# A fused attention, mixer and MLP kernel on one core: the MLP in five blocks of 924 tokens in one pass, with its Strassen weight slices streamed from HBM

## The chip, the core and the metric

The kernel runs on one core of a Trainium2 chip. The metric is the device time of one execution in microseconds (us). Engines are named as in the profile: PE (TensorE matmuls), PEld (its weight loads), DVE (VectorE), ACT (ScalarE), POOL (GpSimd), SP (SyncE, which issues most of the DMAs).

## The reference, cut to what matters

```python
attn_out = _attn_ref(...)                  # feature-map attention, 8 x 8 heads x 576 x 64
x = attn_out.transpose(0, 2, 1, 3).reshape(B, S, H * D)      # 8 x 576 x 512
x = (gate(x) * (x @ w_val)) @ w_out        # gate: sigmoid of a causal convolution of 5 taps
mixed = real(fft(fft(x, axis=1), axis=2))
u = x + mixed
un = (u - mean(u)) / sqrt(var(u) + 1e-6)   # over the 512 features
out = u + maximum(un @ w_ch1, 0) @ w_ch2   # 512 -> 2048 -> 512
```

## The kernel before, in words

**Stages.** The attention (to about 313 us) is scheduled by hand in `run_attention`; beside it the MLP's weights are converted from float64 and written to the HBM scratch `w_scr`. Then come the mixer and the FFT as matmuls ("the mixing", to about 608 us), batch after batch: `note_V` (value, tile `val`), `note_W` (w_out), `note_FD` and `note_SD` (the transforms), which leaves u in the scratch `u_scr`. Then the MLP, to the end.

**Order.** From the mixing on, the functions `note_...`, `ln_stages`, `prep_un`, `c1_units` and `c2_units` only record operations with what they read and write. `place_ops` (line 1112) then plans all of them: each has costs per engine (`COST`, line 617), a due time counted back from the end along its successors and along PE's work, and of the operations that are ready the one due first is placed. Operations recorded for "vp" can go to DVE or POOL. The result is a fixed order of instructions on each engine; each engine runs its own in order. Tiles live in five parts (`STAGES`, line 620) whose memory is opened and closed one after the other.

**Precision.** Every float32 operand is split into a rounded high part and a remainder, and a product takes three float32r matmuls: high by high, high by low, low by high. A split is a copy on ACT (`o_hi`) and a subtraction on DVE or POOL (`o_lo`).

**Strassen.** Both MLP products use a form of Strassen's algorithm with 7 products in place of 8. The weight side needs 7 slices per 2 x 2 quadrant block: three are quadrants themselves and four are sums, which `note_sums` (line 375) computes during the mixing in 32 steps (load of 256 KB, four sums of 128 columns, store of 256 KB; two buffers `ws`). `prep_w` (line 662) later loads them and splits them into resident tiles `w`. The token side needs 7 operands `un`, made by `prep_un` (line 770): 4 sums, 7 high parts, 7 low parts.

**The MLP.** 4608 tokens stand as 9 blocks of 512 (two halves of `HB` = 256 columns). The weights of half the hidden units fit, so there are two passes over the blocks, 18 visits: pass 0 with the first half, partial sums kept in `part_scr` and normalised tokens in `un_scr`, and pass 1 backwards with the other half. A visit has two rounds c. In a round `c1_units` (line 799) has 7 units of 12 matmuls of 256 columns (tiles x, y, z) with the Strassen additions, the ReLU and the splits into `h` after them, 14 vector operations of 512 columns; `c2_units` (line 874) has 7 units of 12 matmuls of 256 columns into cx, cy and cz, each but one added to `acc` on DVE. The c2 of a round runs interleaved with the c1 of the next. In pass 0 the LayerNorm of the next block (`ln_stages`, line 713) runs beside; that of block 0 is recorded in the mixing after batch 4. `note_mlp` (line 1072) records all this.

Of the kernel before, what the change touches and what calls it, by code (L numbers as in the profile page):

```python
# [8 lines left out]
F32 = mybir.dt.float32  # L9
# [11 lines left out]
NT = NB * S  # L21
# [3 lines left out]
TB = 512  # L25
HB = TB // 2
NBK = NT // TB
# [38 lines left out]
def attention_moe_mixer_kernel(  # L66
# [92 lines left out]
    w_scr = [dram.tile([NJ, 2, 128, 8 * 128], F32, name=f"w_scr{i}") for i in range(2)]  # L159
    un_scr = [dram.tile([128, 4, TB], F32, name=f"un_scr{t}") for t in range(NBK)]  # L160
    part_scr = [[dram.tile([128, 2, HB], F32, name=f"part_scr{t}_{q}") for q in range(4)] for t in range(NBK)]
    u_scr = [dram.tile([4, 128, S], F32, name=f"u_scr{b}") for b in range(NB)]

    keep = pool(ctx, "keep", 1)
    wo_all = keep.tile([128, 2, 4 * DM], F32R, name="wo")
    wo = [wo_all[:, i].rearrange("p (c f) -> p c f", f=DM) for i in range(2)]
    P = {"g1": pool(ctx, "g1", 1)}

    mix = ExitStack()
# [22 lines left out]
    late["s1"] = ln_p.tile([128, TB], F32, name="s1")  # L192
    late["A"] = ln_p.tile([128, 4, TB], F32, name="A")
# [176 lines left out]
    def conv_mlp(n, j, i):  # L370
        def done(t):
            nc.sync.dma_start(out=w_scr[i][j][:, :, 0:512].rearrange("o p f -> p o f"), in_=t)
        return convert(n, (w_ch1, w_ch2)[i][j].bitcast(I32).rearrange("o p f -> p o f"), 1024, (2,), False, done)

    def note_sums(n):
        i, j, o = wsteps[n]
        b = ("ws", n % 2)
        t = later(b)
        a21, a11, a12, a22 = (t[:, k * 128:(k + 1) * 128] for k in range(4))
        k21, k11, k12, k22 = keys = [b + (k,) for k in range(4)]  # L380
        o_dma([(t, w_scr[i][j, o][:, 0:512])], [], keys, 256)
        o_tt("vp", a22, a21, a22, ALU.add, 128, [k21, k22], [k22])
        o_tt("vp", a21, a11, a21, ALU.subtract, 128, [k11, k21], [k21])
        o_tt("vp", a11, a22, a11, ALU.subtract, 128, [k22, k11], [k11])
        o_tt("vp", a12, a12, a11, ALU.subtract, 128, [k12, k11], [k12])
        o_dma([(w_scr[i][j, o][:, 512:1024], t)], keys, [("w_scr", i, j, o)], 256)
# [26 lines left out]
    def open_mix():  # L413
# [7 lines left out]
        for i in range(2):  # L421
            late["ws", i] = ws.tile([128, 512], F32, name=f"ws{i}")
            late["pv", i] = psv.tile([128, NE + 2], F32, name=f"val{i}")
            late["gv", i] = P["g"].tile([128, NE], F32, tag="gv", name="gv")
            late["gs", i] = P["g"].tile([128, 2, NE], F32, tag="gs", name="gs")
        late["pa"] = psa.tile([128, 2, 512], F32, name="acc")

    def open_mix2():
# [3 lines left out]
        late["u"] = x2.tile([128, 4, S], F32, name="u")  # L432
        late["u256"] = x2.tile([97, S], F32, name="u256")
# [3 lines left out]
        for i in range(2):  # L437
# [4 lines left out]
            late["T0", i] = x2.tile([128, 2, HB], F32, name=f"T0{i}")  # L442
            late[("sh0", "sl0")[i]] = x2.tile([128, HB], F32R, name=("sh0", "sl0")[i])
        for i in range(4):
            late["ps", i] = ps.tile([128, 512], F32, name=f"ps{i}")
# [12 lines left out]
    wsteps = [(i, j, o) for j in range(NJ) for i in range(2) for o in range(2)]  # L458
# [52 lines left out]
    def note_V(b, m):  # L511
# [4 lines left out]
        for n in range(2):  # L516
# [3 lines left out]
            def prod(e, p=p, sl=sl):  # L520
                ws = slice(m * 128, (m + 1) * 128)
                for c in range(4):
                    mm3(p[:, 0:NE], (wv[0][:, c, ws], wv[1][:, c, ws]), (h[:, c, sl], l[:, c, sl]), c == 0, c == 3)
            op("m", 0, prod, [("xh", c, k) for c in range(4) for k in range(2)], [("pv", n)], 12 * 0.134)
# [21 lines left out]
    NJP = NJ // 2  # L546
    NH_SLOTS = 7
    blocks = [(0, t) for t in range(NBK)] + [(1, t) for t in reversed(range(NBK))]
    wt = [[], []]
    wr = []  # L550
    un_op = []
    hs = []
    h_more = []
# [4 lines left out]
    def w_tiles(p, i, j):  # L558
        return [[p.tile([128, 7, 128], F32R, name=f"w{i}_{j}_{o}_{k}") for k in range(2)] for o in range(2)]

    def w_views(t):
# [908 lines left out]
```

## Time and profile before

| what | us |
|---|---|
| median of 3 runs | 1380.53 (1379.85 to 1385.03) |
| the profiled execution | 1378.82 |
| span of its trace, first to last instruction | 1377.0 |
| PE busy in the span | 1330.1 (97%) |
| DVE busy | 1183.7 (86%) |
| ACT busy | 820.5 (60%) |
| POOL busy | 582.0 (42%) |

The span is what the trace shows; the execution's own time is 1.8 us longer. Busy times are unions of the instructions' durations. On PE a matmul's duration runs on past the start of the next one, so that its pace is read from start to start.

### The profile page before, as it was taken

How to read it: one execution, taken by the hardware profiler on the slowest of the kernel's cores; microseconds unless marked ns; L12 is line 12 of the kernel's file. 1: busy time of each engine (PE TensorE's matmuls, PEld its weight loads, DVE VectorE, ACT ScalarE, POOL GpSimd, SP SyncE). 2: the span in 40 equal slices, each digit the busy share in tenths (PEclk: the TensorE clock that was granted, in tenths of full speed). 3: DMA queues.
4: the chain of work that ended last, by engine and by line, in shares of the span. 5: the costliest groups of instructions: out<-in, count | busy, mean ns of one | idle time of the engine just before them, and what ended most of it. 6: DMA issues, size and time to landing. Idle time of an engine off the chain costs nothing.

```text
span 1377.0 us, 35052 instructions
## 1 busy us (share of the span) xinstructions
PE 1330.1 (97%) x14672; PEld 1288.3 (94%) x14672; DVE 1183.7 (86%) x2006; ACT 820.5 (60%) x1554; POOL 582.0 (42%) x452
## 2 busy tenths in 40 slices
PE   8999999997999999996999999999999999999998
PEld 7888888887999999996999999999999999999998
DVE  7999999887889999887899999999897777777776
ACT  6888888865555546465565565555565445544542
POOL 3978888613666654342533234343223111111110
PEclk9999999998999999998999999999999999999999
DMA  7477777643444440144422333222543212222211
GB/s 266 144 278 272 272 266 263 223 159 121 144 161 161 162 146 35 66 151 167 161 85 85 119 97 123 94 77 77 177 122 105 77 62 78 93 62 92 92 47 46
DMA packets 89849, 186.97 MB, mean 136 GB/s; under 512 B 10454, under 2 KB 37334, under 8 KB 87516
## 3 DMA queue, kind: packets, MB, share of 16 engines
q1 hardware_dynamic: 85312, 174.25, 37.7%
q10 hardware_dynamic: 4380, 10.50, 2.0%
q8 instruction: 115, 1.88, 0.6%
q14 instruction: 42, 0.34, 0.1%
HBM read 121.79 MB, written 62.93 MB: 134 GB/s over the span
## 4 chain that ended last, share of the span: by engine, by line
PE 71%; DVE 21%; ACT 4%; issue 2%; DMA 1%; SPq 0%; POOL 0%; ACTq 0%; DVEq 0%
PE x L62 14%; PE cx L62 13%; PE ps L62 9%; PE cy L62 7%; PE y L62 7%; PE val L62 6%; PE cz L62 4%; DVE y L260 3%; PE z L62 3%; DVE m L257 3%; DVE acc L62 3%; PE kv L62 3%; PE pj L62 3%; PE nm L62 2%; DVE cv L126 2%
## 5 line engine op out<-in xcount | busy, mean ns | idle before, releaser
L62 PE MATMUL cx<-h,w 128*128 128x256 f32 x1260 | 172.9, 283 | 0.6 <-ACT y L62 0.6
L62 PEld LDWEIGHTS cx<-h,w 128*128 128x128 f32 x1260 | 161.1, 191 | 1.0 <-ACT y L62 0.7
L62 DVE TENSOR_TENSOR acc<-cx,acc 128x512 f32<-128x512 f32 x144 | 98.8, 686 | 34.8 <-PE cx L62 34.1
L62 POOL TENSOR_TENSOR un<-A,un 128x512 fp32r<-128x512 f32 x41 | 55.1, 1353 | 172.8 <-ACT un L62 169.2
L62 PE MATMUL val<-xh,wv 128*128 128x290 f32 x768 | 115.7, 306 | 4.7 <-DVE gs L62 2.6
L62 ACT ACTIVATE h<-z 128x512 fp32r<-128x512 f32 x108 | 64.4, 596 | 91.6 <-DVE z L62 91.1
L62 PE MATMUL x<-un,w 128*128 128x256 f32 x864 | 116.6, 285 | 0.4 <-DVE c L62 0.4
L62 PE MATMUL cy<-h,w 128*128 128x256 f32 x792 | 115.2, 282 | 1.2 <-DVE h L62 1.2
L62 PEld LDWEIGHTS val<-xh,wv 128*128 128x128 f32 x768 | 109.6, 196 | 6.6 <-DVE gs L62 3.0
L62 DVE SCALAR_TENSOR_TENSOR acc<-xf,cw,acc 128x576 f32<-128x576 f32 x128 | 105.1, 821 | 10.3 <-ACT acc L62 8.8
L62 PEld LDWEIGHTS x<-un,w 128*128 128x128 f32 x864 | 109.8, 193 | 0.7 <-DVE c L62 0.7
L62 PE MATMUL ps<-ge,wo 128*128 128x290 f32 x768 | 107.0, 297 | 0.6 <-ACT s L62 0.6
L62 PEld LDWEIGHTS cy<-h,w 128*128 128x128 f32 x792 | 105.0, 191 | 1.4 <-DVE h L62 1.4
L62 PEld LDWEIGHTS ps<-ge,wo 128*128 128x128 f32 x768 | 104.2, 189 | 0.8 <-ACT s L62 0.8
L62 POOL TENSOR_TENSOR un<-T,un 128x512 fp32r<-128x512 f32 x42 | 55.1, 1311 | 116.5 <-ACT un L62 116.5
L62 PE MATMUL kv<-vraw,ke 128*64 128x66 f32 x2560 | 94.5, 226 | 0.9 <-DVE kvT L302 0.4
L257 DVE TENSOR_REDUCE m<-pj 128x8 f32<-128x1024 f32 (+1 forms) x80 | 88.5, 1106 | 7.9 <-PE pj L62 7.9
L62 PEld LDWEIGHTS kv<-vraw,ke 128*64 128x64 f32 x2560 | 82.5, 138 | 12.0 <-ACT ke L269 1.1
L62 PE MATMUL pj<-wp,kqraw 64*128 64x128 f32 x1152 | 88.3, 291 | 4.8 <-DMA kqraw<-in_k_dram 4.4
L62 PEld LDWEIGHTS pj<-wp,kqraw 64*128 64x128 f32 x1152 | 72.7, 192 | 18.3 <-issue 18.2
L260 DVE TENSOR_TENSOR y<-pj,m 128x1024 f32<-128x1024 f32 (+1 forms) x80 | 88.5, 1107 | 0.4
L62 PE MATMUL nm<-kvT,qe 128*64 128x65 f32 x2304 | 83.3, 224 | 4.4 <-DVE xs L339 3.3
(200 smaller groups left out, 3515.1 us busy)
## 6 DMA issues: line engine op xcount, KB each, us to landing
raw<-in_w_ch_dram SPq DMA_DIRECT2D x16, 1024.0 KB, 5.8
wr<-w_scr SPq DMA_DIRECT2D x32, 448.0 KB, 3.5
vraw<-in_v_dram SPq DMA_DIRECT2D x16, 660.0 KB, 8.9
x_scr<-xT SPq DMA_DIRECT2D x32, 288.0 KB, 4.1
xf<-x_scr SPq DMA_DIRECT2D x8, 1152.0 KB, 6.5
u_scr<-u ACTq DMA_DIRECT2D x8, 1152.0 KB, 5.7
out_dram<-acc SPq DMA_DIRECT2D x36, 256.0 KB, 2.2
kqraw<-in_k_dram SPq DMA_DIRECT2D x15, 576.0 KB, 6.0
```

What stands on the lines that cost most here:

```text
L62: return lambda *a, **k: f(*(resolve(x) for x in a), **{n: resolve(x) for n, x in k.items()})
L126: nc.vector.tensor_scalar(out=ex, in0=hi32, scalar1=0x7FF00000, scalar2=None, op0=ALU.bitwise_and)
L257: nc.vector.tensor_reduce(out=m, in_=pv, axis=AX.X, op=ALU.max, apply_absolute_value=True)
L260: nc.vector.tensor_tensor(out=y, in0=pv, in1=m.unsqueeze(3).to_broadcast([128, 2, 2 * n, F]), op=ALU.subtract)
```

## The change

The MLP becomes one pass over five blocks: four of 924 tokens (halves of 462 columns) and one of 912. The weights are no longer resident. The 7 slices of each hidden block are kept unsplit in a new scratch `s_scr`, each contiguous, and for every unit of every block one slice is loaded into a ring (10 slots for the first product, 6 for the second) and split there. So `prep_w`, `part_scr` and the resident `w` go, and `note_weights` comes. A c1 unit is 6 matmuls of 462 columns for one j (8 j per block); a c2 unit is 12 matmuls of 462 for two j, and each of its results, 924 columns in two banks, is added to `acc`. `note_sums` has 16 steps of 256 columns with one buffer, whose stores go to `s_scr` in pieces of 512 bytes. Block 0's LayerNorm is done in two halves (`ln_first`) spread over batches 1 to 5 of the mixing; in the planner, operations recorded "in place" (these and the sums) are due no later than the PE work recorded around them, and no operation of a part is due later than the first one of the parts that follow. The LayerNorms of blocks 1 to 4 (`ln_block`) run in the blocks before, from the second pair of the first block on, in a tile `B`, and their means use the c1 banks x0 and x1 (`mean` had its own). The matmuls of `note_V` are recorded as three operations in place of one. The pools of `wo` and `g1` close with the mixing, and `u` moves to the end of its pool.

```diff
-TB = 512
-HB = TB // 2
+HB = 462
+BLOCKS = [(2 * HB * t, HB) for t in range(4)] + [(8 * HB, NT // 2 - 4 * HB)]
...
     def note_sums(n):
+        i, j = wsteps[n]
+        t = later("ws")
+        a21, a11, a12, a22 = (t[:, :, k * 128:(k + 1) * 128] for k in range(4))
+        o_dma([(t, w_scr[i][j].rearrange("o p f -> p o f"))], [], keys, 512)
+        for o in range(2):
+            o_dma([(dst[0:3, :, j % (i + 1), o].rearrange("q p f -> p q f"), v[:, 1:])], keys[1:], [("s", i, j, o, False)], 192)
+        o_tt("vp", a22, a21, a22, ALU.add, 256, [k21, k22], [k22])
...
+            o_dma([(dst[3:7, :, j % (i + 1), o].rearrange("q p f -> p q f"), v)], keys, [("s", i, j, o, True)], 256)
...
+    def note_weights(c, n, first=[]):
...
+        src = s_scr[c][j][q].rearrange("p n k f -> p (n k f)")
+        o_dma([(f32(l), src)], [("s", c, x, o, q > 2) for x in ((j,), (2 * j, 2 * j + 1))[c] for o in range(2)] + first, [lk], (128, 256)[c])
+        o_hi(h, f32(l), cols, [lk], [hk])
+        o_lo(K["w"], l, f32(l), h, cols, [lk, hk], [lk])
...
     def c1_units(t, j):
...
-                for n, j in enumerate(js):
-                    w = wt[0][j % NJP]
-                    for kt in range(2):
+                for kt in range(2):
+                    a, b = w[:, 0, kt], w[:, 1, kt]
+                    for m, (l, v) in enumerate(((a, uh), (a, ul), (b, uh))):
+                        mm(p, l, v[:, kt], start=first and kt + m == 0, stop=kt == 1 and m == 2, skip_group_check=True)
+            note_weights(0, wn[0] - 1 + RING[0])
...
+        SUMS = [(1, 0, 1, 0, 1)] * 5 + [(1, 0, 0, 0, 0), (0,) * 5]
...
-            if b == 4:
-                load_a(0, u_scr)
-                ln_stages(0, K["ln0"])
+            for k in range((0, 1, 2, 2, 1, 1, 0)[b]):
+                in_place(next, ln0, None)
+        drain(ln0)
         b = NB - 2
-        drain(prep_w(0, 0, K["w0"]))
-        drain(prep_w(0, 1, K["w0"]))
+        for n in range(RING[0]):
+            note_weights(0, n)
+        load_first()
...
     def note_mlp():
+        for t in range(len(BLOCKS)):
+            ln = ln_block(t + 1) if t + 1 < len(BLOCKS) else iter(())
+            for pair in range(NJ // 2):
+                c1 = chain(*(c1_units(t, 2 * pair + g) for g in range(2)))
+                for k in range(7):
                     next(c2, None)
+                    next(c1)
+                    next(c1)
+                    if t == 0 and pair == 0 and k == 2:
+                        for n in range(RING[1]):
+                            note_weights(1, n, ["mixed"])
+                        for q in range(4):
+                            load_acc(0, q, ["mixed"])
+                    unit = 2 * pair + k // 4
+                    if k in (1, 5) and unit >= (2 if t == 0 else 1):
+                        next(ln, None)
...
     def place_ops():
...
+                late = min(late, ends[last[i]]) - min(d.values()) - ops[i][4]
                 if "m" in d:
                     now -= d["m"]
                     late = min(late, now)
+                if ops[i][9]:
+                    late = min(late, now)
```

## Rows read from the trace of the kernel before

**Rows 1.** Busy time by stretch: mixing's start, mixing, turn, MLP; us (x instructions)

```profile
core 0: us, PE busy (x) PEld busy (x) DVE busy (x) ACT busy (x) POOL busy (x), PEclk, DMA share, GB/s
313.00:350.00 37.00, 28.02 (x265) 25.02 (x264) 28.29 (x58) 19.92 (x32) 15.85 (x23) 0.84 0.34 114
350.00:600.00 250.00, 248.43 (x1868) 246.40 (x1867) 222.44 (x442) 135.24 (x296) 137.34 (x161) 1.00 0.37 126
600.00:650.00 50.00, 38.06 (x269) 36.27 (x268) 42.48 (x70) 30.05 (x59) 15.67 (x14) 0.86 0.52 174
650.00:1377.00 727.00, 717.72 (x5984) 715.29 (x5983) 606.73 (x969) 385.25 (x691) 191.69 (x155) 1.00 0.29 94
```

**Rows 2.** Busy time by stretch, same columns: attention, steady pass 0, steady pass 1

```profile
100.00:200.00 100.00, 97.09 (x2093) 86.55 (x2091) 94.41 (x158) 84.52 (x159) 83.17 (x34) 1.00 0.77 272
...
865.00:905.00 40.00, 39.64 (x332) 39.47 (x331) 37.02 (x64) 22.87 (x44) 15.02 (x14) 1.00 0.33 106
...
1200.00:1300.00 100.00, 100.00 (x840) 100.00 (x839) 75.10 (x117) 48.08 (x85) 15.58 (x12) 1.00 0.27 86
```

**Rows 3.** Timeline of PE at the turn to the MLP: start, duration, instructions, [idle <-releaser]

```profile
629.84 0.88 PE L62 MATMUL x<-un,wo 128*128 128x256 f32 x6
638.34 0.58 PE L62 MATMUL mean<-sh,ones 128*128 128x256 f32 x1 [7.62 <-ACT sh L62]
...
645.60 1.65 PE L62 MATMUL x<-un,wg 128*128 128x256 f32 x6 [2.29 <-ACT c L62]
```

**Rows 4.** Chain of waits at the turn to the MLP: start, length, what

```profile
629.46 6.51 DMA u_scr<-u
636.02 0.83 issue
636.85 1.13 ACT T L62 x2
```

**Rows 5.** Timeline of PE: matmuls of 128, 290 and 256 columns, back to back

```profile
302.04 1.16 PE L62 MATMUL pj<-wp,kqraw 64*128 64x128 f32 x16
303.13 1.15 PE L62 MATMUL kv<-vraw,ke 128*64 128x66 f32 x32
...
591.14 13.04 PE L62 MATMUL ps<-ge,wo 128*128 128x290 f32 x96
604.01 0.96 PE L62 MATMUL ps<-sq,Y 128*128 128x290 f32 x6
...
1202.29 1.60 PE L62 MATMUL x<-un,w 128*128 128x256 f32 x12
1203.73 1.60 PE L62 MATMUL cy<-h,w 128*128 128x256 f32 x12
```

**Rows 6.** Timeline of DVE in pass 0, operations back to back

```profile
877.75 0.68 DVE L62 SCALAR_TENSOR_TENSOR h<-x,h 128x512 fp32r<-128x512 f32 x1
878.35 0.69 DVE L62 TENSOR_TENSOR y<-c,y 128x512 f32<-128x512 f32 x1
...
894.49 0.42 DVE L62 TENSOR_TENSOR s<-A 128x256 f32<-128x256 f32 x1
894.82 1.43 DVE L62 TENSOR_TENSOR s<-s,A 128x256 f32<-128x256 f32 x4
```

**Rows 7.** Groups of instructions by form: busy us, mean ns, idle before

```profile
L62 ACT ACTIVATE h<-z 128x512 fp32r<-128x512 f32 x108 | 64.4, 596 | 91.6 <-DVE z L62 91.1
L62 POOL TENSOR_TENSOR un<-T,un 128x512 fp32r<-128x512 f32 x42 | 55.1, 1311 | 116.5 <-ACT un L62 116.5
...
L62 DVE RECIPROCAL s<-s 128x128 f32<-128x128 f32 x36 | 33.3, 937 | 0.8 <-ACT s L62 0.8
```

**Rows 8.** The tile ws (Strassen sums) in the mixing: duration ns min/median/max

```profile
L62 POOL TENSOR_TENSOR ws<-ws x102: 449/462/1340, 311.3 to 497.2; 128x128 f32<-128x128 f32 x102
L657 SPq DMA_DIRECT2D ws<-w_scr x32: 319/320/578, 295.8 to 490.0; - x32
...
L62 DVE TENSOR_TENSOR ws<-ws x26: 275/284/531, 352.5 to 498.2; 128x128 f32<-128x128 f32 x26
```

**Rows 9.** DMA issues: transfers, KB each, median us from issue to landing

```profile
wr<-w_scr SPq DMA_DIRECT2D x32, 448.0 KB, 3.5
...
out_dram<-acc SPq DMA_DIRECT2D x36, 256.0 KB, 2.2
```

**Rows 10.** Timeline at the kernel's end: the last c2 unit and its addition

```profile
1371.41 1.66 PE L62 MATMUL cx<-wg,w 128*128 128x256 f32 x12 [0.88 <-DVE acc L62]
1373.11 0.69 DVE L62 TENSOR_TENSOR acc<-cx,acc 128x512 f32<-128x512 f32 x1 [1.84 <-PE cx L62]
```

More of the change, by code (lines that the diff above doesn't have):

```diff
@@ L545, in attention_moe_mixer_kernel @@
     SLOT = (0, 1, 5, 2, 6, 4, 3)
[L546 to L550, printed above, removed]
+    NH_SLOTS = 14
+    RING = (10, 6)
+    ORDER = ((0, 4, 5, 1, 6, 2, 3), (0, 4, 5, 2, 6, 1, 3))
     un_op = []
     hs = []
-    h_more = []
     tl = {}
@@ L630, in stage, with in_place, op @@
         return STAGES.get(n, (0, 4))
-    def op(e, cols, fn, reads, writes, dur=None, more=0.0, two=False):
+    here = [False]
+    def in_place(f, *a):
+        here[0] = True
+        f(*a)
+        here[0] = False
+    def op(e, cols, fn, reads, writes, dur=None, more=0.0, two=False, table=None):
         two = two and not any(k in BANKS or k[0] in BANKS for k in reads)
@@ L639, in op @@
         at = [stage(k) for k in reads + writes]
-        ops.append((dur, fn, reads, writes, more, two, max([a for a, b in at], default=0), min([b for a, b in at], default=4)))
+        ops.append((dur, fn, reads, writes, more, two, max([a for a, b in at], default=0), min([b for a, b in at], default=4), table, here[0]))
+    TABLES = {ACTF.Exp, ACTF.Sigmoid, ACTF.Sqrt}
     def o_hi(dst, src, cols, r, w):
@@ new lines, in ln_half, with ln_first @@
+        split()
+        yield
+        b, p = mean()
+        o_act(s1, p, ACTF.Sqrt, n, [b], ["s1"], bias=eps)
+        for z in range(0, n, 116):
+            x = s1[:, z:min(n, z + 116)]
+            op("v", 0, lambda e, x=x: vec.reciprocal(out=x, in_=x), ["s1"], ["s1"], 0.83)
+        for c in range(2):
+            x = a[:, 2 * c:2 * c + 2]
+            o_tt("v", x, x, s1.unsqueeze(1).to_broadcast([128, 2, n]), ALU.mult, 2 * n, ["s1", ak[c]], [ak[c]])
+        yield
+    def ln_first(k):
+        ak = [("A", c) for c in range(2)]
+        tmp = [("T0", later("T0")), ("sh0", later("sh0")), ("sl0", later("sl0"))]
+        yield from ln_half(tl["A"], ak, k * HB, HB, tmp, lambda: next(ring), K["ln0"])
+        o_dma([(un_scr[k], tl["A"])], ak, [("un_scr", k)], 2 * HB)
@@ L1115, in place_ops @@
         pred = [set() for _ in range(n)]
-        for i, (d, f, r, w, more, two, lo, hi) in enumerate(ops):
+        for i, (d, f, r, w, *more) in enumerate(ops):
             for k in r:
@@ L1157, in place_ops @@
         end = [0.0] * n
-        part = [o[6] for o in ops]
-        last = [o[7] for o in ops]
-        for i in reversed(range(n)):
-            last[i] = min([last[i]] + [last[j] for j in succ[i]])
-            assert part[i] <= last[i], ops[i][2:4]
         left_by = {e: [0] * 5 for e in "mvapd"}
```

492 lines of the change are left out of this document (224 added, 268 removed), and 4 rows, old and new, of the table STAGES.

## The prediction

> **What bounds the kernel now.** I read the busy time by stretch first. From 350 to 600 us and from 650 us to the end PE is busy nearly all the time: 248.4 of 250 us and 717.7 of 727 [rows 1]. So both the mixing and the MLP are bound by PE, and an operation on another engine costs nothing there unless PE waits for it. The turn between them is different: from 600 to 650 us PE has 269 matmuls, at about 0.122 us each some 33 us of work, so 17 us are lost. Two rows of the PE timeline show where: 7.62 us idle ahead of a matmul of `mean`, which is the LayerNorm of block 1, placed ahead of c1's work in PE's order, and 2.29 us for a copy on ACT [rows 3]; the clock's mean of 0.86 [rows 1] is 2.4 GHz with about 14 us at 1.2 GHz after that pause. The chain of waits passes there through the store of u, 6.51 us [rows 4]. Last I looked at DVE and POOL: in pass 0, with LayerNorm beside it, DVE is busy 37.0 of 40 us and POOL 15.0, and PE still 39.64; in pass 1 DVE has 75%, POOL 16% and PE 100% [rows 2].
>
> **PE in the MLP.** Matmul starts are 1.09/16 = 68.1 ns apart at 128 columns, 12.87/96 = 134.1 at 290 and 1.44/12 = 120 at 256 [rows 5]; 840 in 100 us [rows 2] is 119.0, so I take 119.4. At 2.4 GHz the columns alone are 53.3, 120.8 and 106.7. What is left, 14.8, 13.3 and 12.7 ns, doesn't grow with the columns: each matmul costs some 13.5 ns beside its columns. A matmul of 462 is then 192.5 + 13.5 = 206.0 ns, one of 456 is 203.5. Before: 18 visits x 2 rounds x 14 units x 12 = 6048 matmuls x 0.1194 = 722.1 us. After: each block has 8 x 7 x 6 + 4 x 7 x 12 = 672, in four blocks 2688 x 0.2060 = 553.7 and in the last 672 x 0.2035 = 136.8, together 690.5. The term is **-31.6 us**, all on the path. No row has 462 columns. Were the excess 12.7 ns, it would be -34. Were it proportional to the columns (134.1/290 = 0.462 ns per column), the MLP would take 716 and the term would be -6. I take the fixed cost, since the row at 128 columns contradicts a proportional one (59 ns against 68.1).
>
> The Trainium skill (TensorE: Matmul & The Clock Gate, "Back-to-back issue gap") gives columns / 2.4 GHz plus 2.5 ns for a warm matmul. By it the 2688 matmuls saved would be worth only 6.7 us, and this sum would come out near 1375. The trace doesn't agree: by that rule 256 columns would take 109.2 ns, and they take 119.4.
>
> **DVE and POOL in the MLP.** On DVE 512 columns take 0.60 us from start to start, 256 take (1.43 - 0.42)/3 = 0.34 [rows 6], so 462 take 0.55 and 924 take 1.03; POOL takes 1.31 for 512 [rows 7], 2.18 times as much. All sums here are in DVE time.
> Before, pass 0, two rounds (40.1 us of PE): 52 operations of 512 (26 per round: 13 of c1, 6.5 additions to `acc`, one low part, 5.5 of `prep_un`) = 31.2, and a LayerNorm: 8 of 512, 4 reciprocals of 0.94 [rows 7], 16 of 256 = 14.0. That is 45.2, or 1.13 of PE's time; pass 1 has 0.78.
> After, per j (84 matmuls, 17.3 us of PE): 13 of 462 and 3.5 of 924 on DVE alone = 10.8; LayerNorm there 1.03 + 0.85 = 1.9; for either engine one low part 0.55, `prep_un` 11 x 1.03 / 8 = 1.4, the low parts of the weights 7 x 0.34 + 3.5 x 0.60 = 4.5, LayerNorm 16 x 0.55 / 8 = 1.1. Together 20.2, or **1.17** of PE's time in blocks 0 to 3; in block 4, without LayerNorm and `prep_un`, 15.9, or 0.92.
> So halving `prep_un` saves less than splitting every slice in every block costs, and four fifths of the MLP carry slightly more than pass 0 did. Pass 0 lost 0.36 of 40 us [rows 2], 1%; 1% of 554 us is 5 us. The most that rows show of the two engines in a long stretch is the mixing, 222.4/250 + 137.3/250/2.18 = 1.14 [rows 1]; at this limit a j takes 20.2/1.14 = 17.7 us, and 32 j lose 14. I take 14, less the 5 that the MLP idles now (727 - 717.7, less 4 after the last matmul): **+9 us**. Ends: 0, and the caps of pass 0 (0.925 + 0.375/2.18 = 1.10), 18.4 us per j, +35.
>
> **ACT and DMA: nothing.** ACT has per j 14 copies of 462, 7 of 924 per 8 j, 7 of 256 and 3.5 of 512; at 0.596 for 512 [rows 7] and in proportion that is 12.6 us of 17.3. Its reserve covers that; without it a late high part delays the low part behind it. The rings load 280 x 128 KB + 140 x 256 KB = 73 MB, while 48 MB for partial sums, `un_scr` and `wr` go: about 136 GB/s in place of 94, against 272 GB/s in the attention [rows 1, 2]. A load lands in 2.2 to 3.5 us [rows 9], and a ring holds 24 us of work or more. SP issues 420 loads at 0.32 us [rows 8], 134 of 690 us. The new wait is on SP: the six first loads of the second ring and four of `acc` wait for the end of the mixing, and the refills of the first ring stand behind them; PE has ten slices by then, 12 us of work, so a delay shows only beyond that.
>
> **The turn.** Block 1's LayerNorm, and so the wait of 7.62, moves behind the first pair; 14.0 us of its vector work go. `u` is now the last tile of its pool, so that by the order of allocation `h` no longer waits for its store [rows 4]. Against that, `prep_un` takes 11 x 1.03 = 11.3 in place of 6.6, and the first pair has c1 alone: 17.3 us of PE against 28 x 0.55 + 14 x 0.34 + 6 x 0.60 = 23.8 of vector work, at 1.14 some 4 us late. I take a loss of 10 in place of 17: **-7**. Ends: -17, and +10 if the late start stretches into another pause with the clock at 1.2 GHz.
>
> **The mixing and the end.** LayerNorm of 924 tokens in place of 512 adds 10 us to DVE; the sums have half as many operations and give back some 5. DVE is at 89% there while PE has 248.4 of 250 [rows 1]: hidden; without PE's cover it costs 5 to 10. One `ws` buffer makes a step a chain: load 3.7, first store 2.5, four sums of 0.34 to 0.74, second stores 3, so 11 to 14 us and for 16 steps 180 to 220 of the 270 us before that memory closes. The loads of x stand behind these stores in SP's queue, with a batch (34 us) to spare. The three records of `note_V` issue the same matmuls: 0, within 2 us either way. At the end the last addition has 912 columns (+0.4) and the last store 456 KB lands like 448 KB, 3.5 against 2.2 [rows 9], while the wait of 0.88 goes [rows 10]: **+0.8**. `mean` has 40 matmuls of 462 in place of 72 of 256, 8.2 us in place of 8.6: 0.
>
> **Sum**, against the profiled 1378.8: -31.6 + 9 - 7 + 0.8 = **1350 us**. The median of the runs is 1.7 above that execution, which I leave out.
>
> **Rivals.**
> 1. *POOL can't take its share* (the slower side). To need no more than 17.3 us per j with DVE at 0.93, POOL must do 0.24 in DVE time, 52% busy; it is at 37.5% in pass 0 and 16% in pass 1 [rows 2]. For it: POOL and DVE stretch each other when both work in SBUF, 1340 against 462 ns and 531 against 284 on the same shape [rows 8], and all low parts are of that kind. Against it: POOL reached 55% in the mixing beside a DVE at 89% [rows 1]. At 37.5% the time is 1350 - 9 + 35 = 1376; at 30% a j takes 19.0 and the time is 1395; at 16%, 1434. It decides below 37%.
> The Trainium skill (SBUF — State Buffer, "Who interferes with whom") says that a DVE operation with two SBUF inputs and a POOL operation that reads SBUF exclude each other for a whole instruction; the stretched rows agree.
> 2. *The cost per matmul grows with the columns*: -6 in place of -31.6, so 1375. Against it stands the row at 128 columns [rows 5]. The rule of the first page above comes to the same time and shares this chance.
> 3. *The turn gets worse*: +10 in place of -7, so 1367. The vector work ahead of the first pair speaks for it, the LayerNorm that leaves against it.
> 4. *The change doesn't do what it says*: slices arrive late because SP's queue is blocked. One pause of 8 us per block as in [rows 3] would give 1390. The rings' 24 us speak against it.
>
> **Chances.** My forecast 0.52, with its own range of 1338 to 1364; rival 1 0.26, half of it between 1364 and 1379 and half slower; rival 2 0.08; rival 3 0.08; rival 4 0.06. A measurement of this kernel tells about 0.5% from no change, that is 7 us. Faster: 0.52 + rival 3's 0.08 + half of rival 1's first half and of rival 2, 0.11 = 0.71. Within it: the other halves and a part of rival 4 = 0.13. Slower: 0.16. The range of 1334 to 1380 leaves out some 0.16 above and a few hundredths below.
>
> **What would show it.** Matmuls of 462 about 206 ns apart; from 700 us on DVE above 90% and POOL at 45 to 55% in blocks 0 to 3, both lower in block 4; no pause of 7 us for `mean`; waits of PE in the MLP of some 14 us, most of them behind DVE. It is wrong if the matmuls are 213 apart, if POOL stays below 37%, or if the mixing ends later than 608 us.

## The result and the profile after

The change takes 1369.83 us (median of 5 runs, 1366.38 to 1372.48), the kernel before 1380.53 (5 runs beside them, 1378.49 to 1385.03). The ratio is 0.9918, with an interval of 0.9903 to 0.9934: faster by 0.8%, clear of the noise, and a third of what was forecast. The profiled execution took 1368.61 us with a span of 1366.8, so the two profiled executions differ by 10.2 us.

The busy time by stretch of the kernel after answers to [rows 1], with the same columns and the end of the MLP at 1367:

```profile
core 0: us, PE busy (x) PEld busy (x) DVE busy (x) ACT busy (x) POOL busy (x), PEclk, DMA share, GB/s
313.00:350.00 37.00, 30.60 (x320) 27.85 (x316) 33.46 (x75) 21.22 (x34) 7.88 (x10) 0.91 0.48 153
350.00:600.00 250.00, 236.34 (x1750) 231.19 (x1749) 232.86 (x441) 132.26 (x275) 107.02 (x83) 1.00 0.46 145
600.00:650.00 50.00, 46.84 (x309) 43.84 (x308) 42.10 (x70) 33.91 (x82) 30.41 (x22) 1.00 0.58 190
650.00:1367.00 717.00, 701.69 (x3316) 623.58 (x3314) 601.69 (x855) 484.79 (x1012) 423.84 (x403) 1.00 0.45 134
```

Read against [rows 1], the surprise is the second line. In the mixing, which the forecast left alone, PE fell from 248.4 to 236.3 of 250 us, while DVE rose from 222.4 to 232.9. The turn improved from 38.1 to 46.8 of 50. In the MLP POOL took 424 of 717 us, 59%, and DVE 84%.

The waits of PE from 350 to 603 us in the kernel after (engine, tile waited for, releaser: us in total, times, longest):

```profile
PE ps L61 <- DVE Y L61: 5.3, 5, 1.5
PE val L61 <- DVE gs L61: 3.5, 3, 1.3
PE val L61 <- DVE gv L61: 2.6, 2, 2.0
PE ps L61 <- DVE x L61: 1.0, 1, 1.0
PE ps L61 <- POOL f L61: 0.6, 1, 0.6
PE ps L61 <- DVE rem L61: 0.6, 1, 0.6
```

That is 13.6 us in 13 waits (the view leaves out short ones), nearly all behind DVE; the same view of the kernel before has 1.5 us in three. `gs`, `gv` and `Y` are the mixing's own small products, which PE needs next.

The timeline of PE in the kernel after answers to [rows 3] and [rows 5]: the last batch's product with W, the turn, back-to-back matmuls of 462 columns, and the last ones of 456.

```profile
603.17 13.04 PE L61 MATMUL ps<-ge,wo 128*128 128x290 f32 x96
...
637.91 2.38 PE L61 MATMUL x<-un,r 128*128 128x462 f32 x10 [1.17 <-DVE r L61]
641.27 1.54 PE L61 MATMUL x<-un,r 128*128 128x462 f32 x6 [0.98 <-DVE c L61]
643.82 1.53 PE L61 MATMUL x<-un,r 128*128 128x462 f32 x6 [1.00 <-ACT c L61]
...
677.75 1.42 PE L61 MATMUL x<-un,r 128*128 128x462 f32 x6
679.01 2.67 PE L61 MATMUL cy<-h,r 128*128 128x462 f32 x12
...
1356.97 2.64 PE L61 MATMUL cy<-h,r 128*128 128x456 f32 x12
1359.45 2.67 PE L61 MATMUL cx<-h,r 128*128 128x456 f32 x12
```

Three readings. The block of 96 starts at 603.17 where it started at 591.14 [rows 5]: the mixing ends 12.0 us later, and the transforms behind this block, which ended at 608.0, end at 620.1. The turn has three waits of about 1 us where one of 7.62 and one of 2.29 stood [rows 3]. And six matmuls of 462 columns take 679.01 - 677.75 = 1.26 us, 210 ns each, where 206.0 had been forecast.

One more pause stands out in the MLP. The timeline of the kernel after at the passage from block 0 to block 1:

```profile
765.72 0.99 PE L61 MATMUL cy<-h,r 128*128 128x462 f32 x4
...
766.23 2.15 DVE L61 TENSOR_TENSOR B<-B,s 128x924 f32<-128x924 f32 x2
...
768.29 1.12 DVE L61 TENSOR_TENSOR A<-B 128x924 f32<-128x924 f32 x1
...
769.33 0.63 DVE L61 TENSOR_TENSOR h<-y,h 128x462 fp32r<-128x462 f32 x1
...
770.56 3.13 PE L61 MATMUL cy<-h,r 128*128 128x462 f32 x8 [3.84 <-DVE h L61]
```

Three LayerNorm operations of 924 columns, 3.2 us from 766.23 on, stand ahead of a low part `h` that PE waits for. The matmuls behind the pause run at 1.2 GHz for 3.4 us (the granted clock halves from 771.0 to 774.4), and from 750 to 800 us PE loses 6.4 us in all.

Where the 10.2 us are, in PE's time: I added up, over all matmuls, the distance from start to start beyond the back-to-back distance of that shape.

| place | forecast | measured |
|---|---|---|
| MLP's matmuls: 2688 x 210.5 + 672 x 207.5 ns = 705.3 us against 722.1 | -31.6 | -16.8 |
| the mixing, to the last product with W | 0 | +12.0 |
| the turn: 4.5 us lost (620 to 651) against 16.7 (608 to 651) | -7 | -12.2 |
| waits in the MLP: 15.6 against 8.6 | +9 | +7.0 |
| the end | +0.8 | 0 |
| sum | -28.8 | -10.0 |

210.5 and 207.5 are means over the back-to-back matmuls of the MLP. The row of the mixing is a balance: by the same sum PE loses 18.3 us from 350 us to the last product with W, against 3.6 before, and the passage from the attention gives a part of that back (PE is busy 30.6 us from 313 to 350, before 28.0).

### The profile page after: what moved, and what is told of

It reads as the page before. It is cut to its first block, busy times and chain, and to the rows that moved or that the text cites. A ratio compares the mean times of both kernels' runs of the same rounds, so it can differ in the third digit from the quotient of the medians.

```text
span 1366.8 us, 30765 instructions
## 1 busy us (share of the span) xinstructions
PE 1312.9 (96%) x11952; PEld 1191.6 (87%) x11952; DVE 1191.5 (87%) x1905; ACT 921.7 (67%) x1876; POOL 788.8 (58%) x615
## 4 chain that ended last, share of the span: by engine, by line
PE 61%; DVE 27%; ACT 4%; DMA 4%; issue 2%; SPq 1%; POOL 0%; DVEq 0%; ACTq 0%; POOLq 0%
PE cx L61 13%; PE x L61 12%; PE cy L61 9%; PE y L61 6%; PE ps L61 6%; DVE acc L61 3%; DVE y L258 3%; PE val L61 3%; PE z L61 3%; PE kv L61 3%; DVE m L255 3%; PE pj L61 3%; PE nm L61 2%; DMA s_scr<-ws 2%; DVE cv L125 2%
## 5 line engine op out<-in xcount | busy, mean ns | idle before, releaser
L61 POOL TENSOR_TENSOR r<-r 128x256 fp32r<-128x256 f32 (+1 forms) x320 | 304.5, 970 | 202.6 <-ACT r L61 178.6
L61 PE MATMUL x<-un,r 128*128 128x462 f32 (+1 forms) x960 | 225.3, 373 | 5.4 <-ACT c L61 2.9
L61 ACT ACTIVATE r<-r 128x256 fp32r<-128x256 f32 (+1 forms) x420 | 194.1, 487 | 41.6 <-DMA r<-s_scr 39.4
L61 PE MATMUL cx<-h,r 128*128 128x462 f32 (+1 forms) x960 | 214.8, 372 | 2.2 <-DVE acc L61 1.5
L61 PEld LDWEIGHTS x<-un,r 128*128 128x128 f32 x960 | 180.1, 188 | 28.6 <-ACT c L61 4.5
L61 PEld LDWEIGHTS cx<-h,r 128*128 128x128 f32 x960 | 180.1, 188 | 24.4 <-DVE acc L61 2.7
L61 PE MATMUL cy<-h,r 128*128 128x462 f32 (+1 forms) x720 | 161.9, 373 | 3.8 <-DVE h L61 3.8
L61 PEld LDWEIGHTS cy<-h,r 128*128 128x128 f32 x720 | 136.0, 189 | 19.9 <-DVE h L61 4.4
L61 PE MATMUL val<-xh,wv 128*128 128x290 f32 x768 | 116.7, 304 | 11.9 <-DVE gv L61 6.6
L61 PE MATMUL y<-un,r 128*128 128x462 f32 (+1 forms) x480 | 114.5, 373 | 2.0 <-DVE h L61 1.9
L61 PEld LDWEIGHTS y<-un,r 128*128 128x128 f32 x480 | 90.1, 188 | 14.2 <-DVE h L61 4.0
```

What stands on the lines that cost most here:

```text
L61: return lambda *a, **k: f(*(resolve(x) for x in a), **{n: resolve(x) for n, x in k.items()})
```

## The experiments

**The price of a matmul of 462 columns, by itself.** One kernel with PE almost alone: blocks of 96 matmuls, and beside them one short DVE copy per block.

```
for s, n in enumerate((512, 128, 192, 256, 290, 320, 384, 462, 512, 256, 462)):
    for i in range(96):
        nc.tensor.matmul(p[:, 0:n], xr[:, 128*(i % 3):128*(i % 3) + 128], xr[:, 512:512 + n], ...)
```

> PE alone: 96 matmuls of each size back to back, a new weight load ahead of each, no other engine working; everything else of the computation is left out. In the changed kernel matmuls start 210.5 ns apart at 462 columns and 207.5 at 456, in both kernels 134.2 at 290, before 119.4 at 256. Theory A: a float32r matmul costs 6 ns and 0.442 ns per column whatever goes on beside it; then 128 takes 63, 192 91, 384 176, 462 210.5 and 512 232.5. Rival B, the term of the prediction (13.5 ns and 1/2.4 ns per column), with the MLP's traffic as what slowed the 462: alone 462 takes 206, 512 226.8, 384 173.5, 128 67. Rival C, in proportion to the columns: 128 takes 59.5, 512 238. The same in bfloat16 at 256, 462 and 512 shows whether the slope belongs to the four-byte operand: A expects 1/2.4 ns per column there, 207 or less at 462.

The timeline of PE in this kernel (start, duration of the block):

```profile
28.87 10.83 PE L49 MATMUL p1n<-xr 128*128 128x128 f32 x96
39.54 10.91 PE L49 MATMUL p2n<-xr 128*128 128x192 f32 x96
50.29 11.70 PE L49 MATMUL p3n<-xr 128*128 128x256 f32 x96
...
88.71 16.83 PE L49 MATMUL p6n<-xr 128*128 128x384 f32 x96
105.38 20.48 PE L49 MATMUL p7n<-xr 128*128 128x462 f32 x96
125.69 21.95 PE L49 MATMUL p8n<-xr 128*128 128x512 f32 x96
...
179.32 10.66 PE L54 MATMUL h0n<-b 128*128 128x256 bf16 x96
189.81 18.88 PE L54 MATMUL h1n<-b 128*128 128x462 bf16 x96
208.53 20.88 PE L54 MATMUL h2n<-b 128*128 128x512 bf16 x96
```

From start to start, float32r matmuls take 111.7 ns at 128 and at 192 columns, 120.0 at 256, 173.3 at 384, 211.7 at 462 and 226.7 at 512. Columns / 2.4 + 13.3 gives 120.0, 173.3 and 226.7, so a fixed cost beside the columns is right at these sizes, and both theories of a cost that grows (A: 63 at 128, 176 at 384 and 232.5 at 512; C: 238 at 512) fail. But 462 would be 205.8 by it, and is 5.8 above without the MLP's traffic, so the second half of theory B fails too. In bf16 256, 462 and 512 columns take 109.2, 195.0 and 215.8. The Trainium skill (TensorE: Matmul & The Clock Gate, "Back-to-back issue gap") gives columns / 2.4 + 2.5 for a warm matmul; the bf16 blocks agree within 0.1 ns, the float32r blocks are 10.0 ns (at 290 columns) or more above it.

**Which sizes are dear.** The same with eighteen sizes from 400 to 512, and with one unchanging weight tile.

> PE alone again, 96 matmuls of each of 18 sizes from 400 to 512 columns, the weights changing with each; then 462 and 448 with one unchanging weight tile. The first run of this kind gave 120.0 at 256, 146.7 at 320, 173.3 at 384 and 226.7 at 512, all 13.3 ns + columns/2.4, but 211.7 at 462, 5.8 more, with starts that vary from 202 to 220 in a pattern. Theory: some sizes cost more than that line, and those that are multiples of 32 don't: 416, 448 and 480 lie on it (186.7, 200.0, 213.3), 456 and 462 some 4 to 6 ns above. Rival 1: the excess rises smoothly from 384 and falls to 512; then 448 has 4 or more. Rival 2: it comes with the size of 4 bytes x columns against 64 bytes (multiples of 16 columns free, 464 on the line at 206.7). With one weight tile the excess stays if it is of the moving operand and goes if it is of the weight loads.

Four of its blocks, and one with the weights unchanging:

```profile
161.57 20.19 PE L49 MATMUL pi456x<-xr 128*128 128x456 f32 x96
181.60 20.03 PE L49 MATMUL pj460x<-xr 128*128 128x460 f32 x96
201.47 20.48 PE L49 MATMUL pk462x<-xr 128*128 128x462 f32 x96
221.79 20.22 PE L49 MATMUL pl464x<-xr 128*128 128x464 f32 x96
...
368.34 20.48 PE L54 MATMUL one0n<-xr 128*128 128x462 f32 x96
```

The excess over columns / 2.4 + 13.3 ns is 0 at 400 and 512, 1.7 at 460, 5.8 at 462, 2.2 at 464, 5.5 at 456, 9.1 at 488 and 3.3 at 504. It follows neither multiples of 16 or 32 nor a smooth curve, and it is the same with one unchanging weight tile, which is still loaded ahead of each matmul. Every theory of its cause that I had stated fell; the cause is open, the prices are measured.

**A cheaper size.** Blocks of 464 columns, and then the LayerNorm begun one unit earlier as well:

```
-HB = 462
+HB = 464
...
-                    if k in (1, 5) and unit >= (2 if t == 0 else 1):
+                    if k in (1, 5) and unit >= 1:
```

> The changed kernel with halves of 464 columns in blocks 0 to 3 and of 448 in the last, nothing else edited (the planner orders anew). In the sweep on an idle chip 464 columns took 208.9 ns and 448 202.7, against 211.6 at 462 and 208.9 at 456. Theory (the pace belongs to the size of the matmul): the MLP's 3360 matmuls come down from 2688 x 210.5 + 672 x 207.5 = 705 us to about 2688 x 208 + 672 x 202 = 695, and the time by 8 to 12 us, with the mixing and the turn within 4 us of the changed kernel's. Rival (the excess over 13.3 ns + columns/2.4 in the kernel is traffic from other engines): 464 takes 211 or more and the time doesn't fall.

> The same with block 1's LayerNorm recorded from the second unit of block 0 on, as in the other blocks, and not from the third. In the changed kernel PE waits 3.8 us at 766 to 770 us for a low part of h that stands on DVE behind the reciprocals and the last step of that LayerNorm, and then runs 3.4 us at 1.2 GHz, 6 to 7 us in all from 750 to 800. Theory: this pause goes, and with the sizes of the run before the time is 1368.6 - 10 - 6 = 1353, ratio to the kernel before 0.98. Rival: the LayerNorm that starts earlier brings back a pause at the turn (650 to 700 us) of the same size, and the time stays at that of the run before.

The matmuls came close to the price list: 209.2 and 203.5 ns (the last block has 448 columns), where the same count gives 210.3 and 207.8 in the change, so some 6 us less in all. The time did not follow: 1377.96 us in one run with 464 alone, and 1372.07 (1368.3 to 1373.2, ratio 0.9924 with 0.9907 to 0.9941) with the earlier LayerNorm. The order written for other costs put other things first: the mixing ended 4 us later in the first, and while the earlier LayerNorm did remove the pause at 770 us (6.4 us lost there became 1.4), another stands in the last block, in the run with 464 alone as well. Its timeline in the second kernel:

```profile
1208.84 8.61 POOL L61 TENSOR_TENSOR r<-r 128x256 fp32r<-128x256 f32 x10
...
1210.44 7.95 DVE L61 TENSOR_TENSOR un<-A,un 128x896 fp32r<-128x896 f32 x1
...
1218.45 2.24 PE L61 MATMUL x<-un,r 128*128 128x448 f32 x5 [4.39 <-DVE un L61]
1219.26 1.08 DVE L61 TENSOR_TENSOR un<-A,un 128x896 fp32r<-128x896 f32 x1
```

The same operation that takes 1.08 us at 1219.26 took 7.95 at 1210.44, and ended 0.9 us after a row of ten operations on POOL. The Trainium skill (SBUF — State Buffer, "Who interferes with whom") says that a DVE instruction with two SBUF inputs contends with a POOL instruction that reads SBUF, and that whoever issues first keeps the shared ports for the whole instruction. This row agrees. In it DVE's operation ended only after the last of POOL's ten.

**What makes the mixing late: the same work left out of a new order.** First the sums were dropped and block 0's LayerNorm was dropped, each with the order written anew:

```
 def note_sums(n):
...
-        o_tt("vp", a22, a21, a22, ALU.add, 256, [k21, k22], [k22])
...
-        yield from ln_half(tl["A"], ak, k * HB, HB, tmp, lambda: next(ring), K["ln0"])
+        from_u(tl["A"], k * HB, HB, w=ak)
```

> The changed kernel without the four Strassen sums of each of the 16 steps; their loads and stores stay. The output is left wrong by that. Theory: in the mixing (350 to 603 us) PE waits 18.2 us, before 3.4, because DVE is full: the sums take 27.0 us of DVE there (before 7.6, with POOL 40.0, now 9.6) and block 0's LayerNorm takes some 13 us more than before. Without the sums DVE falls from 233 to about 206 of 250 us, PE's waits there fall to 8 or less and the time by about 10 us. Rival: the chain of one ws buffer (load, sums, stores; its DMAs are 13% of the chain of waits from 440 to 530 us) holds up the mixing; then the waits stay above 14.

> The changed kernel without block 0's LayerNorm in the mixing (its tokens go into the MLP unnormalised; load and store stay). Theory of a full DVE: about 24 us of DVE go, from 233 to about 210 of 250, and PE's waits from 350 to 603 us fall from 18 to 8 or less, as without the sums, so that the two don't add up. Rival, that the sums alone do it: the waits fall by less than 5.

Without the LayerNorm the time is 1355.99 us (one run of each), W starts at 588.6 and PE is busy 247.1 of 250 us; without the sums it is 1366.29. But there the new order let the mixing keep 11.4 us of waits and added 10 us between 599 and 617 us, where a store of `un_scr` came late. A kernel whose order is planned answers a removal with another order, so these two can't be read as prices.

**The same work left out of the order as it is.** The planner sees the operations and places them; then they are not issued.

```
+    mute = [False]
...
-        ops.append((dur, fn, ...
+        ops.append((dur, (lambda e: None) if mute[0] else fn, ...
```

> The changed kernel in its own planned order, with the four Strassen sums of each step not issued (the output is left wrong by that); unlike the first try without the sums nothing else is planned anew. Theory of a full DVE: in the mixing DVE falls by some 25 us, PE's waits from 350 to 603 us fall from 18.2 to 9 or less, and the mixing's last w_out block starts 6 to 9 us earlier than at 603.2. Rival (the order itself holds PE up, whatever DVE has to do): the waits stay above 14.

> The same with block 0's LayerNorm not issued, but its loads and stores (the MLP gets block 0 unnormalised), in the order planned for the changed kernel. Theory of a full DVE: about 24 us of DVE go, the waits from 350 to 603 us fall to 10 or less. Rival (the sums alone): by less than 4.

> Both left out, same order. If a full DVE is the cause, little more than the better one of the two single cases: waits of 3 to 6 us from 350 to 603, like the 3.4 before the change, and W of the last batch starting at about 589 to 592 us. If waits of 10 or more stay, the order is the cause.

Busy time by stretch from 350 to 600 us. Without the sums:

```profile
350.00:600.00 250.00, 243.17 (x1818) 239.56 (x1817) 219.85 (x411) 137.92 (x290) 98.30 (x71) 1.00 0.50 159
```

without block 0's LayerNorm:

```profile
350.00:600.00 250.00, 240.19 (x1783) 235.92 (x1782) 217.03 (x421) 124.01 (x274) 103.67 (x81) 0.99 0.47 151
```

and without both:

```profile
350.00:600.00 250.00, 246.78 (x1856) 244.23 (x1855) 197.14 (x384) 131.90 (x288) 98.55 (x71) 1.00 0.50 158
```

In the mixing PE gets back 6.8 us from the sums, 3.9 from the LayerNorm and 10.4 from both, of the 12.1 that it lost there, so the two add up. W of the last batch starts at 595.7, 598.0 and 586.9, where it was 603.2 (without the LayerNorm its eight matmuls, some 1.7 us of PE, are gone too); the times are 1361.60, 1364.00 and 1353.98 us (one run each). DVE, ACT and POOL have their other operations in the same order as in the change, so both parts cost. The theory of a full DVE is not borne out as it was stated. Of the 18.3 us lost to 603 us, 9.7, 14.8 and 5.2 are left, where at most 9, at most 10 and 3 to 6 had been expected; the LayerNorm alone gives 3.5, which is the rival's "less than 4". And without it DVE is busy 217 of 250 us, less than the 222 before the change, while PE still has 8 us less than then. The sums are dearer than their size: their 43 DVE operations from 350 to 600 us took 27.0 us, 629 ns each, in the kernel after. The tile's row there answers to [rows 8] (ns, min/median/max):

```profile
L61 DVE TENSOR_TENSOR ws<-ws x51: 405/417/1674, 323.1 to 599.7; 128x256 f32<-128x256 f32 x51
...
L61 POOL TENSOR_TENSOR ws<-ws x13: 735/739/751, 361.2 to 584.6; 128x256 f32<-128x256 f32 x13
```

In the kernel before DVE had 26 of them and 7.65 us from 350 to 600, POOL 82 and 40.1. In their new form (twice the size, one buffer, a due time by place) the planner gave the sums to DVE, the engine with the least room. Operations of DVE more than 150 ns over their form's median add up to 13.5 us in that stretch, against 5.3 before and 6.8 without the sums. The sums themselves are 9.0 of it: eight of the 43 took 1.2 to 1.7 us, and each of the eight ran beside a low part, of `xh` or `f`, on POOL.

**Giving the sums back to POOL.** Once by forcing all of them there, once by their old form, half as wide, with two buffers and without the due time by place, by which the planner shares them as before.

```
-        o_tt("vp", a22, a21, a22, ALU.add, 256, [k21, k22], [k22])
+        o_tt("p", a22, a21, a22, ALU.add, 256, [k21, k22], [k22])
...
-    wsteps = [(i, j) for j in range(NJ) for i in range(2)]
+    wsteps = [(i, j, o) for j in range(NJ) for i in range(2) for o in range(2)]
```

> The changed kernel with the Strassen sums recorded for POOL alone (the planner orders anew). In the changed kernel 43 of them take 27.0 us of DVE from 350 to 600 us, stretched from 417 to 629 ns on average; without them, in the same order, PE waited 8.7 us less. Theory: on POOL they take 64 x 0.74 = 47 us, of which DVE bears only the lock, and PE's waits from 350 to 603 us fall from 18.2 by 4 to 8 us. Rival: a step's chain of four sums gets 1.3 us longer on POOL and with one buffer the steps end later, so that the mixing's end waits for them; then the waits only move, and the time stays within 3 us of 1368.6 or rises.

> The changed kernel with the Strassen sums in the form they had before: 32 steps of 128 columns, two buffers, five steps per batch, not due by place; the stores go to the new scratch as in the change. In their planned order the changed kernel's sums cost 8.7 us of PE's waits in the mixing and block 0's LayerNorm 3.5. Theory: the larger steps with one buffer and an early due time are what brought the sums onto DVE; in the old form POOL takes most of them again (before 82 of 108 from 350 to 600 us), DVE's share of them falls below 12 us, PE's waits from 350 to 603 us fall from 18.2 to 10 or less, and the time by 6 to 9 us. Rival: DVE is full with block 0's LayerNorm of 924 tokens alone; the waits stay above 13.

Forced onto POOL, the chain of sums ends late, the memory closes late, and the time is 1388.55 us (one run), with 8.6 us of loss at 603 to 620 and 11.9 from 620 to 655. In the old form (1370.20 us in one run) the row of the stretch is

```profile
350.00:600.00 250.00, 240.26 (x1763) 235.57 (x1762) 223.27 (x423) 132.93 (x273) 139.32 (x165) 0.98 0.47 151
```

DVE and POOL are back at 223.3 and 139.3 us, as before the change (222.4 and 137.3 [rows 1]), and PE still loses 8 us more than then; W starts at 604.0. So the busy share of DVE over the whole stretch doesn't decide, and the form of the sums is not the cause alone. What POOL takes over makes its own work late: the longest wait is now 3.8 us for a low part of `xh` on POOL, at 480 us. The waits lie between 450 and 550 us, where the LayerNorm of block 0 has its place. There DVE is busy 95.3 of 100 us in the kernel after and PE 92.3; before the change they were at 92.0 and 99.4.

Two combinations that should have beaten both kernels, the old form of the sums with the earlier LayerNorm and blocks of 464 or 460 columns (for 460, four of 460 and a last one of 464):

```
-HB = 462
-BLOCKS = [(2 * HB * t, HB) for t in range(4)] + [(8 * HB, NT // 2 - 4 * HB)]
+HB = 464
+HN = 460
+BLOCKS = [(2 * HN * t, HN) for t in range(4)] + [(8 * HN, NT // 2 - 4 * HN)]
```

> The run before, with halves of 464 and 448 columns and block 1's LayerNorm recorded from the second unit on. Sizes: 208.7 and 203.3 ns in place of 210.5 and 207.5, 2688 x 1.8 + 672 x 4.2 = 8 us; pause at 750 to 800 us gone, 5 to 6 us. From the time of the sums in the old form 13 us less, so some 1349, if the new order brings no pause of its own; with the pause that the first run of 464 had in the last block (4.6 us and the slow clock), 1356.

> The same with halves of 460 columns in blocks 0 to 3 and of 464 in the last. On an idle chip 460 took 206.7 ns, 4.9 less than 462. Then the MLP's matmuls take 2688 x 206 + 672 x 208.7 = 694, 11 us less than in the change; with the pause at 750 to 800 and the sums' 8 us gone the time is 1368.6 - 11 - 6 - 8 = 1344, with a new pause of the order up to 1354. Faster than both kernels either way.

They take 1371.58 us (ratio 0.9926, 0.9904 to 0.9947) and 1368.56 (0.9908, 0.9884 to 0.9932). Neither can be told from the change. In the second a matmul of 460 columns took 208.7 ns in the kernel, not the 206.7 of the block by itself, and what the matmuls gave (some 4 us) came back from 603 to 651 us, where PE loses 9.4 us against 4.6 in the change. In the kernel 456, 460, 462 and 464 columns lie within 3 ns of each other (207.8, 208.7, 210.3, 209.2), so a price taken alone holds there to 1 or 2 ns. No version that beats the change was found.

**The turn.** Five runs asked what held PE 16.7 us there in the kernel before. In the change, `u` was put back to its old place:

```
+        late["u"] = x2.tile([128, 4, S], F32, name="u")
+        late["u256"] = x2.tile([97, S], F32, name="u256")
         late["fs"] = x2.tile([128, 2, NE], F32, name="fs")
```

> The changed kernel with u and u256 allocated second in their pool, as before the change. At the turn (620 to 651 us) PE loses 4.5 us over its pace, before 16.7. Theory: most of this gain is that h no longer lies where u is still being stored (6.51 us in the chain before); then the loss rises to 10 or more and the time by 5 to 8 us. Rival: the gain is block 1's LayerNorm, which left the turn; then the loss stays under 7.

1370.94 us (one run), and the turn still loses 4.6: in the change the place of `u` is worth nothing. In the kernel before, the LayerNorm of block 1 was moved behind the first unit, or left out with the order kept:

```
-                    if c == 0 and i == (3 if bi == 0 else K["lnat"]) and ps == 0 and t + 1 < NBK:
+                    if (c, i) == ((1, 3) if bi == 0 else (0, K["lnat"])) and ps == 0 and t + 1 < NBK:
```

> The kernel before, with block 1's LayerNorm recorded in round 1 of block 0 and not in round 0, the one edit. At the turn (608 to 651 us) it loses 16.7 us, the changed kernel 4.5; u at its old place in the pool changed nothing. Theory: what left the turn is that LayerNorm; then its loss falls to 8 or less. Rival: it is the rest of what stands there (the splits of the resident weights and the operands un of block 0, and the planner's due times); then 12 or more is lost, with another wait in place of the one for mean.

> The kernel before in its own order, with the LayerNorm of block 1 not issued, its DMAs kept (block 1 goes unnormalised into the MLP). The turn (608 to 651 us) loses 16.7 us there. Recording this LayerNorm later moved the wait (12.7 and 5.8 more after it). Theory: the LayerNorm in the turn is the cause of the pause, through PE's fixed order and DVE's time; with it gone and nothing else planned anew the loss falls to 5 or less, near the changed kernel's 4.5. Rival: the weights' splits and the store of u; then 10 or more is lost.

Moved, it takes 1383.57 us (one run); the wait for `mean` is still there, 8.3 us, and the turn loses 12.8. Left out (with the mute of above around block 1's stages), it takes 1376.83 (one run) and the turn loses 14.6 us: the next matmul waits 9.3 us in its place. The LayerNorm stood at the wait and didn't make it. Then the place of `u` was changed in the kernel before, alone and together with the LayerNorm left out:

```
-        late["u"] = x2.tile([128, 4, S], F32, name="u")
-        late["u256"] = x2.tile([97, S], F32, name="u256")
         late["fs"] = x2.tile([128, 2, NE], F32, name="fs")
...
             late[("sh0", "sl0")[i]] = x2.tile([128, HB], F32R, name=("sh0", "sl0")[i])
+        late["u"] = x2.tile([128, 4, S], F32, name="u")
+        late["u256"] = x2.tile([97, S], F32, name="u256")
```

> The kernel before with one thing of the change: the tiles u256 and u come last in their pool. The orders of all engines are those of the kernel before. The turn (608 to 651 us) loses 16.7 us of PE in the kernel before and 4.5 us in the change (620 to 651). Theory: what holds the turn in the kernel before is the memory below u; the ACT copy that fills a weight tile waits 5.12 us for the last store of u, and the copy that feeds the matmul of mean stands behind it in ACT's queue. With u elsewhere that wait goes: the turn loses at most 10 us, the wait for mean falls below 3 us, and the time is 6 to 10 us less than before, 1370 to 1374. Rival: the wait moves to another tile that lies on u or behind DVE's work on block 1's LayerNorm: the turn still loses 14 us or more and the time is within 3 us of before.

> The kernel before, in its own order, with both parts of the turn taken at once: the LayerNorm of block 1 is not issued, as in before_ab (its output is therefore not the reference's), and u256 and u come last in their pool, as in before_ulast. Alone the first left 14.6 us of PE's loss from 608 to 651 us and the second 14.1, of 16.7. Theory: the two hide each other. In before_ab the longest wait (9.3 us, for DVE c) comes from the copy that fills a weight tile on ACT and waits 5.2 us for u's last store; in before_ulast it is the LayerNorm's mean and the work around it. With both gone the turn loses at most 8 us and the time is 1366 to 1372, 9 us or more below before. Rival: what is left is neither, but the weights' own splits on ACT and DVE and their loads: the turn still loses 11 us or more and the time is 1373 to 1376.

What this was to remove is a wait of ACT in the kernel before:

```profile
635.99 0.95 ACT L62 ACTIVATE w<-wr 128x896 fp32r<-128x896 f32 x1 [5.12 <-DMA u_scr<-u]
```

Alone it takes 1377.3 us (median of 12 runs; ratio 0.9971, 0.9961 to 0.9981): a real gain of 4 us, below the 6 to 10 of the theory, and the turn still loses 14.1. The ACT copy no longer waits for the store of `u`, the wait for `mean` falls from 7.62 to 2.39 us, and the wait behind it grows from 2.29 to 3.60. With both it takes 1377.14 (one run) and the turn still loses 13.2, which is the rival's "11 us or more". The timeline of that last kernel, on SP's queue, ACT and PE:

```profile
610.25 10.70 SPq L658 DMA_DIRECT2D wr<-w_scr  x4
629.96 3.19 SPq L658 DMA_DIRECT2D acc<-u_scr  x4
633.25 11.63 SPq L658 DMA_DIRECT2D wr<-w_scr  x4
...
639.51 0.95 ACT L62 ACTIVATE w<-wr 128x896 fp32r<-128x896 f32 x1 [3.59 <-DMA wr<-w_scr]
...
642.33 1.65 PE L62 MATMUL x<-un,wg 128*128 128x256 f32 x6 [5.18 <-ACT c L62]
```

and its chain of waits:

```profile
632.48 0.77 DVE w L62
633.25 6.24 DMA wr<-w_scr
```

The load of the next weight slice is issued at 633.25, behind four loads of `acc` and just as DVE ends the split of an earlier slice; the chain passes 6.24 us of that DMA, ACT's copy waits for it, `c` stands behind that copy in ACT's queue, and PE waits for `c`. By this chain the turn was held by the weights' path, two `wr` buffers, their loads on SP's queue and their splits on ACT and DVE, with the store of `u` as one link; no run changed that path alone in the kernel before. In the change that path is another: SP issues 18 loads of finished slices from 603.35 on, 21 us before the first matmul of c1. SP's timeline in the kernel after:

```profile
603.35 36.03 SPq L653 DMA_DIRECT2D r<-s_scr  x18
639.47 1.21 SPq L653 DMA_DIRECT2D acc<-u_scr  x1
```

## Where the forecast was wrong, and what of it held

The sign was right and the time lies in the wider range of 1334 to 1380, but above the forecast's own 1338 to 1364: 10.7 us were gained for 30.5. Two steps carry the difference.

**"A matmul of 462 is then 192.5 + 13.5 = 206.0 ns"** is the term that was mis-sized: -31.6 forecast, -16.8 measured. The mechanism was right, a fixed cost per matmul that fewer, wider matmuls save, and the runs show it, 13.3 ns, at 256, 384, 400 and 512 columns. But the price isn't a straight line between those sizes: alone, 462 and 456 columns are among the dear ones, 5.8 and 5.5 ns over it, and in the kernel 3360 matmuls x 4.4 ns over the forecast make the 14.8 us. The rival of a cost that grows with the columns would have given -6 and was wrong in its mechanism; the forecast named 213 ns as the sign of its failure, and 210.5 came. The ground on which it was set aside was luck, though. The 16 matmuls of 128 columns at 302.04 [rows 5] have weights of 64 rows and start in eight pairs, 6 or 7 ns apart within a pair and some 111 ns from pair to pair; 68.1 is no price of one matmul, and with 128 x 128 weights 128 columns take 111.7.

**"DVE is at 89% there while PE has 248.4 of 250 [rows 1]: hidden"** is the step that failed: 0 forecast, +12.0 measured. The cover was named and its price without it, 5 to 10 us, was stated; the cover wasn't there: PE's small operands stand in DVE's fixed order behind the added work, whatever the busy share. The mixing that ends after 608 us is also one of the three signs by which the forecast called itself wrong. With both kinds of work left out of the same order PE gets 10.4 of 12.1 us back, so it is shown that they cost it. That the sums would "give back some 5" was wrong twice: they went from POOL to DVE (7.65 us on DVE became 27.0), and they stretch there, by 9.0 us. How the rest divides between the length of one LayerNorm operation and its place is open, since no run changed its place alone.

**The turn** was forecast at -7 with an end at -17, and gave -12.2. The reason given was partly wrong. Of the LayerNorm's removal the runs show 2.1 us at the turn, of the place of `u` 2.6, and of both together 3.5; what waited for the store of `u` was the copy into a weight tile, not `h`. What is left in the last run waits on the weights' path, which the change replaces and which the forecast didn't list. That the new path alone makes the rest of the gain was not tried, and stays open.

**The waits of the MLP**, +9 forecast and +7.0 measured, come out by another way than the one given. Busy times of the kernel after in blocks 0 to 3 and in block 4 (columns as above):

```profile
700.00:1220.00 520.00, 511.43 (x2413) 454.52 (x2412) 452.00 (x632) 367.51 (x759) 337.56 (x315) 1.00 0.45 134
1230.00:1360.00 130.00, 129.89 (x625) 117.03 (x624) 95.62 (x146) 75.80 (x161) 47.22 (x50) 1.00 0.39 118
```

In blocks 0 to 3 DVE is at 87%, not above 90, and POOL at 65%, above the 45 to 55 named. Added as in the forecast, 0.87 + 0.65/2.18 is 1.17: the demand was sized rightly, but the two engines do it with PE at 98%, so 1.14 was no limit, and the loss taken from it came near by luck. Of the 15.6 us 6.4 are one pause, at the passage from block 0 to 1. The first rival, a POOL that can't take its share, is refuted by the 65%. The fourth rival's pause of 8 us per block didn't come; PE waited 1.17 us for the split of a slice once, at 637.91. The end cost nothing that can be told apart.

## What to carry to other kernels

Measure a matmul at the exact size that is planned: between two known sizes the price can lie several ns off the line, and 3360 matmuls made 15 us of it. In an order that is fixed, a busy share below 100% is no cover: ask which small operation the bound engine needs next, and what stands ahead of it in the queue. And take work out of the order as it is before you take it out of the program; a planner answers the second with another order, and its waits are not the price of the work.

## What was not expected of the hardware

- Float32r matmuls alone on PE at 2.4 GHz, with 128 x 128 weights, take columns / 2.4 + 13.3 ns at 256, 384, 400 and 512 columns, 111.7 at both 128 and 192, and between 416 and 504 columns 1.6 to 9.1 ns more than that line, without a pattern that I could name.
- Matmuls with weights of 64 rows start in pairs in the kernel before, 6 or 7 ns apart, so that the mean distance of starts is not the price of one.
- In bf16 462 columns take 195.0 ns, without that excess.
- One DVE operation of 1.1 us took 7.95 while POOL ran ten in a row, and PE paid 4.4 us for it.
- In the kernel before, the order in which two tiles are allocated is worth 4 us, with every instruction in its old place.
